# Moving a unit's mask to GpSimd, its steps to the end of a head pair, and a group's sums off VectorE

## The chip, the cores and the metric

One core of a Trainium2 chip runs the whole kernel in one launch. The metric is the device time of that core in microseconds (us); less is better. Engines are called as the profile calls them: PE (TensorE matmul), PEld (its weight loads), DVE (VectorE), ACT (ScalarE), POOL (GpSimd), SP (the engine that issues the DMAs). Each engine works through its own instructions in program order, and waits for the others by semaphores.

## The reference

Three stages follow each other: attention with a decay, an MLP with h·cos(h), and a mixture of experts whose gates are normalised by eight Sinkhorn rounds.

```python
def _attn_ref(q, k, v, f):                     # q, k, v: 4 x 8 x 576 x 64
    scores = scale * np.matmul(q, k.transpose(0, 1, 3, 2))
    cum = np.cumsum(np.log(np.clip(f, 0.0001, 1.0)), axis=-1)
    decay = cum[:, :, :, None] - cum[:, :, None, :]
    scores = np.where(causal, -1000000000.0, scores + decay)
    scores = scores - np.max(scores, axis=-1, keepdims=True)
    attn = np.exp(scores)
    attn = attn / (np.sum(attn, axis=-1, keepdims=True) + 1e-09)
    return np.matmul(attn, v)

def _moe_ref(x, w_in, w_out):                  # x: 2304 x 512, w_in: 512 x 2048
    h = x @ w_in
    return (h * np.cos(h)) @ w_out

def _moe2_ref(x, w_gate, w1, w2):              # 8 experts of width 1024
    P = np.exp(logits - logits.max())          # logits = x @ w_gate
    for _ in range(8):
        P /= P.sum(1, keepdims=True) + 1e-09
        P /= P.sum(0, keepdims=True) + 1e-09
        P *= N / E
    for e in range(E):
        out += P[:, e:e + 1] * (np.maximum(x @ w1[e], 0.0) @ w2[e])
    return out
```

## The kernel before, in words

The order of all work is written out by hand (`tc.manual_schedule()`): for each engine the program's order is the order in which Python issues instructions.

**Attention.** The 32 heads go in 16 pairs. A pair has seven steps (PS = 7), and the loop over x runs through them: step y = x % 7 works on three pieces of the first head's rows, three of the second's, and one with the last 64 rows of both. A step issues on PE transposes (`turn`, L699), scores three steps ahead (L642, L643), transposes of q and k of the next pair (L522) and products with v (`weigh`, L751, L731); on ACT the exponentials (L687), the high halves `A` (L713) and the high parts of q and k (L536, L538); on DVE the row limits `nm` (L681), the low halves `A` (L721), the low parts of q (L547) and the norms (L759 to L771); on POOL the low parts of k (L599, L552), the split of v (L503 to L507) and rows of the finished output (`split_row`, L242, L165, L166). Scores run as sums of products of high and low parts, so Q1 and Q2, K1 and K2 are the first and second operand of a head (four of each, in turn); `clear` fills the rows and columns that the heads leave empty with zeros and ones.

**Units.** The weights of the MLP come in 16 units, each with two halves of 128x512. They are raw double-precision words that are made into fp32 by integer work: `read_unit` has for each half three DVE steps (L189, L191, L194), a mask step that sets tiny values to zero (L197, with `dm`, the squared word from POOL, L175), and an ACT step that sums squares (L200). Then `scale_unit` adds up over the partitions (a matmul, L133, then L138 and three small POOL steps), and `split_unit` scales (ACT, L217) and splits into high and low halves (POOL, L165, L166). Units are Python generators: one `next(pieces)` goes one step further. Three and a half units are made during attention; the loop there decides at which x a step is taken (`turn_`), and `quiet` at which x a unit's matmul may go to PE. The other units are made between the items of the MLP.

**MLP.** An item is one 128-wide tile of the hidden layer for one chunk of tokens: 12 matmuls into `ph` (L281), ACT and DVE work (L296 to L312) that gives `H`, and two items later 12 matmuls with `H` into `a` (L1015). At the end of a block of items the four banks of `a` are emptied into `acc`, in the first block of the hidden layer by ACT (L1031).

**Experts.** Tokens go in three groups of 768. A group's operand is seven blocks of sums and differences (`combine`: sums L1424, high halves by ACT L1436, low halves by POOL L1439), planned at numbered hooks (`put_at`); 28 hooks make one group's pass through a layer pair. For the second group (p = 1) four of the eight sums run on DVE.

Of the kernel before, what the change touches and what calls it, by code (L numbers as in the profile page):

```python
# [17 lines left out]
ALU = mybir.AluOpType  # L18
# [5 lines left out]
def kernel(  # L24
# [13 lines left out]
    nc = tc.nc  # L38
# [9 lines left out]
    LAST = QT[-1][1]  # L48
# [26 lines left out]
    def f32(ap):  # L75
        return ap.bitcast(F32)
# [95 lines left out]
    def guard(n):  # L172
        if n < len(jobs):
            top = words_of(n)[2]
            nc.gpsimd.tensor_tensor(dms[n % 2], top, top, ALU.mult)  # L175

    def tm_of_unit(u):
        return u % 2 if u < NWA + 1 else (u - NWA + 1) % 3

    def read_unit(u):  # L180
        tm, ws = tmw[tm_of_unit(u)], wsum[u % 3]
        for half in range(2):
            n = 2 * u + half
            top, low, _ = words_of(n)
            x = tm[:, half * DM : (half + 1) * DM]
            xi = x.bitcast(I32)
            if n == 0:
                guard(0)
            nc.vector.tensor_scalar(xi, top, 3, 0x3FFFFFFF, ALU.logical_shift_left, ALU.bitwise_and)  # L189
            yield  # L190
            nc.vector.scalar_tensor_tensor(xi, top, -0x40000000, xi, ALU.bitwise_and, ALU.bitwise_or)  # L191
            guard(n + 1)
            yield
            nc.vector.scalar_tensor_tensor(xi, low, 29, xi, ALU.logical_shift_right, ALU.bitwise_or)  # L194
            load_job(n + 2)
            yield
            nc.vector.scalar_tensor_tensor(x, dms[n % 2], TINY * TINY, x, ALU.is_ge, ALU.mult)  # L197
            yield
            out_ = W[u % NSLOT][:, 0, half * DM : (half + 1) * DM] if late_[0] else junk[0][:, 0:DM]
            nc.scalar.activation(out_, x, AF.Square, accum_out=ws[:, half : half + 1])  # L200
        yield

    def scale_unit(u):
        while not quiet[0]:
            yield
        ps = total(wsum[u % 3], 0)
        if late_[0]:
            yield
        yield from make_scale(ps, sc_w[:, u], bk_w[:, u])
        nc.gpsimd.tensor_tensor(both[:, u : u + 1], bk_w[:, u, 0:1], bk_w[:, u, 1:2], ALU.mult)  # L210
        yield
# [12 lines left out]
        yield from scale_unit(u)  # L224
        yield from split_unit(u)

    late_, quiet = [False], [True]
    BATCHES = [(c0 // S, (c0 + n - 1) // S) for c0, n in CH]

    def chunk_scale(j):  # L230
# [84 lines left out]
    with tc.manual_schedule():  # L315

        with ExitStack() as actx:
# [83 lines left out]

            def clear(eng, i):
                other = QL[1 - i % 2]
                for t, rows_, value in (
                    (Q2, slice(D, P), 0.0), (K2, slice(D, P), 0.0), (Q2, slice(D, D + 4), -1.0), (K2, slice(D, D + 4), 1.0),
                ):
                    eng.memset(f32(t[i])[rows_, :], value)
                    yield
                for t in (Q1, Q2):
                    eng.memset(f32(t[i])[:, other : other + LAST], 0.0)  # L410

            def step(gen, n=1):
                for _ in range(n):
                    next(gen, None)
# [5 lines left out]
            nc.vector.memset(kraw[0][LAST:P, NQ - 1, :], 0.0)  # L420
            nc.vector.memset(quarter, 0.25)
            nc.vector.memset(shift, HALF_PI)
            step(clears[0], 2)
            make_identity(nc, ident)
            nc.gpsimd.memset(segm, 1.0)
            seg3 = segm.rearrange("p (g r) -> p g r", r=SEG)
# [5 lines left out]
                out=seg3, in_=seg3, compare_op=ALU.is_ge, fill=0.0, base=-1,  # L432
                pattern=[[SEG, NHEAD], [1, SEG]], channel_multiplier=-1,
            )
            step(clears[1], 5)


            nc.vector.tensor_scalar(fr, fr, 0.0001, 1.0, ALU.max, ALU.min)
# [10 lines left out]
            )  # L449
            nc.sync.dma_start(cumd.rearrange("r p s -> p r s"), f32(cum))  # L450
            step(clears[0])
            step(clears[2], 3)
            load_v(0)
            aug(0)
            load_pair(1)
# [14 lines left out]
            def pad_v(i):  # L470
                nc.gpsimd.memset(vraw[i][:, :, :, D : D + 1], 1.0)
                nc.gpsimd.memset(vraw[i][LAST:P, NQ - 1, :, :], 0.0)

            def pads():
                nc.gpsimd.memset(ones, 1.0)
                pad_v(0)
                nc.gpsimd.memset(qraw[1][0:LAST, NQ - 1, D : 2 * D], 0.0)
                nc.gpsimd.memset(qraw[1][LAST:P, NQ - 1, 0:D], 0.0)
                for t in (kraw[1], xpt):
                    nc.gpsimd.memset(t[LAST:P, NQ - 1, :], 0.0)  # L480
                for t in v_hi:
                    nc.gpsimd.memset(t[:, :, :, D : D + 1], 1.0)
# [391 lines left out]
            for x in range(-9, NSTEP + PS):  # L874
                for n, when in enumerate((NSTEP - 2, NSTEP + 1)):
                    if x == when:
                        ahead[n] = layer1(*items[n])
                quiet[0] = x % PS in (1, 2, 4, 5) or x >= NSTEP
                on_pe(x)
                if x == NSTEP + 2:  # L880
                    first = begin(*items[0], ahead[0])
                    core(first, None)
                    next(pieces, None)
                    core(None, first)
                    next(pieces, None)
                on_act(x)
                on_dve(x)
                if x == -7:
                    step(clears[2])
                go("pool", x)  # L890
                if x == -5:
                    pads()
                if x == -4:
                    step(clears[2])
                if x == -2:
                    more_pads()
                for j, (_, b1) in enumerate(BATCHES):
                    if x == (HP * b1 + HP - 1) * PS - 3:
                        scaling = chain(scaling, chunk_scale(j))
                turn_ = (x + 1) % 2 if x % PS != 3 else 0  # L900
                if x % PS == 4:
                    turn_ = 1
                if x >= 4 and (turn_ or x >= NSTEP - 8):
                    next(pieces, None)
                if x % 2 or x >= NSTEP - 8:
                    next(scaling, None)
                if rows and rows[0][0] <= x:
                    split_row(*rows.pop(0)[1:])
                if x == NSTEP - PS - 2:
                    block_factors(0)  # L910
                if x == NSTEP - PS - 1:
                    for u in range(NWA):
                        turn_factors(u, 0, 3)
                if x == NSTEP - 3:
                    assert not list(scaling)
                    for u in range(NWA):
                        turn_factors(u, 3, NCH)
                    down_factors(0, 0, NCH)
# [494 lines left out]
        def combine(p, rooms):  # L1413
# [6 lines left out]
                src[B11, k], src[B21, k], src[B22, k] = acc[:, k, t0], acc[:, 2 + k, t0], acc[:, 2 + k, t1]  # L1420

            def sub(dst, a, b):
                eng = nc.vector if p == 1 and k == 1 else nc.gpsimd
                return lambda: eng.tensor_tensor(dst, a, b, ALU.subtract)  # L1424

            sums = []
            for k in range(2):
# [12 lines left out]

            order = [(c, k) for c in (B11, B21, T2, T1, T3, B22, T4) for k in range(2)]
            if p == 1:
                order = [(c, k) for cs in ((B11, B21), (T2, T1), (B22, T3, T4)) for k in range(2) for c in cs]
            return sums, [high(*x) for x in order], [low_(*x) for x in order]

        def bank(kind):
# [248 lines left out]
        def plan_groups():  # L1695
            sums, highs, lo_ = combine(1, xtmp + [t[:, c : c + HN] for t in tmps for c in (0, DM)])
            for n, x in zip((1, 2, 4, 5), (0, 2, 1, 3)):
                put_at(n, lambda x=x: scale_group(1, x))
            for n, fn in zip((2, 3, 4, 5, 14, 15, 16, 17), sums):
                put_at(n, fn)  # L1700
            for n in range(14):
                put_at(10 + n, highs[n])
# [102 lines left out]
```

## Time and profile before

| | |
|---|---|
| median of 3 runs | 1970.86 us (1969.96 to 1970.99) |
| the profiled execution | 1973.44 us, its span 1971.7 us |
| busy in the span | PE 1930.4, DVE 1478.3, ACT 1214.0, POOL 1108.5 us |
| mean granted clock of TensorE | 0.996 |
| attention | about 13 to 242 us of the span |
| MLP | to about 636 us |
| experts | to the end |

The span runs from the first to the last instruction; the execution's own time is 1.74 us longer. Rows give start and duration; in brackets stands how long the engine sat idle before an instruction, and which engine's work ended that wait. "PEclk" is the clock granted to TensorE as a share of full speed (1.00 is the level of 2.4 GHz, 0.50 that of 1.2 GHz).

### The profile page before, as it was taken

Reading aid. Unit: us, or ns where it says so; the run is one execution under the profiler, and the core shown is the slowest. Engines: PE = TensorE matmul, PEld = TensorE weight load, DVE = VectorE, ACT = ScalarE, POOL = GpSimd, SP = SyncE. Lnnn points to the kernel's source line nnn. Section 1 sums busy time; section 2 is a strip of 40 time slices with the busy share of each in tenths; the row PEclk is TensorE's granted clock in tenths of the full one; section 3 lists DMA queues with packets and bytes.
Section 4 is the critical chain, followed back from the end, with each engine's and each line's share of the span. In section 5 each row is a group of like instructions: output and inputs, shape, how many; then the busy total and the mean of one; then the engine's idle time right before and its main releaser. Section 6 shows DMA issues by size and latency. Waiting matters only on the chain.

```text
span 1971.7 us, 38837 instructions
## 1 busy us (share of the span) xinstructions
PE 1930.4 (98%) x14490; PEld 1379.8 (70%) x14490; DVE 1478.3 (75%) x3271; ACT 1214.0 (62%) x2449; POOL 1108.5 (56%) x1546
## 2 busy tenths in 40 slices
PE   7999999999999999999999999999999999999998
PEld 6788855454455677777777777777777777777776
DVE  7888877787577678887777777777777777777776
ACT  6989888777644775655555555555555655556543
POOL 6778864333085785555555555555555555555531
PEclk8999999999999999999999999999999999999999
DMA  5454255453402022202122021220202202122022
GB/s 124 97 114 112 66 171 182 150 170 120 148 22 79 22 82 86 79 22 89 33 78 78 23 89 33 78 78 22 89 33 78 79 22 89 33 78 78 12 89 65
DMA packets 133916, 157.51 MB, mean 80 GB/s; under 512 B 63840, under 2 KB 98016, under 8 KB 133728
## 3 DMA queue, kind: packets, MB, share of 16 engines
q1 hardware_dynamic: 133728, 155.03, 25.8%
q8 instruction: 114, 1.87, 0.4%
q14 instruction: 74, 0.61, 0.1%
HBM read 139.71 MB, written 10.37 MB: 76 GB/s over the span
## 4 chain that ended last, share of the span: by engine, by line
PE 81%; DVE 8%; ACT 7%; issue 2%; DMA 1%; POOL 0%; SPq 0%; DVEq 0%; ACTq 0%; POOLq 0%
PE y L1670 19%; PE y L1549 18%; PE bq L1670 14%; PE bq L1549 14%; PE ph L281 6%; PE a L1015 6%; DVE A L721 1%; ACT E L687 1%; ACT A L713 1%; ACT seen L966 1%; DVE t L309 1%; DMA seen<-in_moe_w_dram 1%; DVE E L681 1%; PE pss L642 1%; ACT t L296 1%
## 5 line engine op out<-in xcount | busy, mean ns | idle before, releaser
L1670 PEld LDWEIGHTS <-h 128*128 128x128 f16 x6048 | 591.5, 98 | 74.9 <-issue 0.9
L1549 PEld LDWEIGHTS <-wa 128*128 128x128 f16 x4032 | 394.2, 98 | 257.1 <-issue 3.0
L1549 PE MATMUL y<-xc,wa 128*128 128x384 f16 x2304 | 429.6, 326 | 1.7 <-ACT ct L1565 1.0
L1584 POOL TENSOR_TENSOR h<-rt,h 128x384 f16<-128x384 f32 x192 | 175.4, 914 | 451.3 <-ACT h L1583 444.3
L1670 PE MATMUL y<-wb,h 128*128 128x256 f16 x3456 | 408.7, 273 | 0.0
L1565 ACT ACTIVATE ct<-y 128x384 f32<-128x384 f32 x192 | 94.4, 492 | 423.2 <-PE y L1549 423.0
L1549 PE MATMUL bq<-xc,wa 128*128 128x384 f16 x1728 | 327.9, 326 | 0.2 <-ACT ct L1565 0.2
L1670 PE MATMUL bq<-wb,h 128*128 128x256 f16 x2592 | 306.7, 273 | 0.2 <-DVE h L1575 0.2
L1651 DVE SCALAR_TENSOR_TENSOR acc<-y,gate,acc 128x256 f32<-128x256 f32 x504 | 212.7, 478 | 48.6 <-PE y L1670 48.6
L1015 PE MATMUL a<-H,w 128*128 128x512 f16 (+1 forms) x960 | 201.3, 358 | 4.0 <-DVE H L312 1.8
L281 PE MATMUL ph<-xt,w 128*128 128x512 f16 (+1 forms) x960 | 199.8, 358 | 0.0
L1651 DVE SCALAR_TENSOR_TENSOR acc<-bq,gate,acc 128x256 f32<-128x256 f32 x378 | 159.7, 478 | 39.2 <-PE bq L1670 39.1
L1015 PEld LDWEIGHTS <-w 128*128 128x128 f16 x960 | 93.4, 98 | 99.8 <-issue 7.8
L1575 DVE TENSOR_TENSOR h<-bq,h 128x384 f16<-128x384 f32 x288 | 158.2, 551 | 3.2 <-ACT h L1572 0.6
L1569 DVE SCALAR_TENSOR_TENSOR bq<-bq,ct 128x384 f32<-128x384 f32 x192 | 107.7, 561 | 65.2 <-PE bq L1549 64.4
L281 PEld LDWEIGHTS <-w 128*128 128x128 f16 x960 | 93.3, 99 | 88.8
L1569 DVE SCALAR_TENSOR_TENSOR bq<-y,ct 128x384 f32<-128x384 f32 x96 | 54.4, 566 | 122.1 <-PE y L1549 119.2
L1572 ACT CAST h<-bq 128x384 f16<-128x384 f32 x288 | 134.8, 484 | 14.2 <-DVE bq L1626 14.0
L1578 POOL TENSOR_TENSOR h<-st,h 128x384 f16<-128x384 f32 x96 | 87.9, 916 | 85.3 <-ACT h L1572 82.7
L309 DVE SCALAR_TENSOR_TENSOR t<-ph,turnv,t 128x512 f32<-128x512 f32 (+1 forms) x80 | 55.6, 695 | 96.1 <-ACT t L296 95.9
L1582 ACT ACTIVATE rt<-bq 128x384 f32<-128x384 f32 x192 | 93.8, 488 | 21.1 <-DVE bq L1569 18.4
L1327 POOL TENSOR_TENSOR tm<-sg 128x256 f32<-128x256 f32 x128 | 92.1, 731 | 13.5 <-POOL h L1578 12.3
(269 smaller groups left out, 3270.6 us busy)
## 6 DMA issues: line engine op xcount, KB each, us to landing
xc<-xd SPq DMA_DIRECT2D x105, 384.0 KB
seen<-in_moe_w_dram SPq DMA_DIRECT2D x64, 512.0 KB
sg<-in_moe_w_dram SPq DMA_DIRECT2D x64, 512.0 KB
stg<-in_moe_w_in_dram SPq DMA_DIRECT2D x16, 512.0 KB
stg<-in_moe_w_out_dram SPq DMA_DIRECT2D x16, 512.0 KB
xd<-xc SPq DMA_DIRECT2D x14, 384.0 KB
q<-q SPq DMA_DIRECT2D x30, 160.0 KB
out_dram<-acc SPq DMA_DIRECT2D x18, 256.0 KB
```

Of the source, the lines that this page charges most:

```text
L281: nc.tensor.matmul(ps[:, 0:n], w[:, ws, kk * P : (kk + 1) * P], XT[j][:, xs, kk, :], start=first, stop=kk == KD - 1 and (ws, xs) == PASSES ...
L1015: nc.tensor.matmul(a_of[b, j][x][:, 0:n], w[:, s1, DM + x * P : DM + (x + 1) * P], H[:, s2, 0:n], start=i == 0 and n_ == 0, stop=end and n ...
L1327: return [lambda o=o, x=x, y=y, op=op: nc.gpsimd.tensor_tensor(o, x, y, op) for o, x, y, op in todo]
L1549: nc.tensor.matmul(ps[:, 0:HN], w[:, ws, a, k, :], X[b][:, xs, k, :], start=fresh and n == 0, stop=n == 5, skip_group_check=not fresh,)
L1565: nc.scalar.activation(c, cut(ps), AF.Copy, scale=RAISE)
L1569: nc.vector.scalar_tensor_tensor(cut(c), cut(ps), RAISE, other, ALU.mult, ALU.add)
L1572: nc.scalar.copy(HT[m][c][:, 0, :], src)
L1575: nc.vector.tensor_tensor(HT[m][c][:, 1, :], src, HT[m][c][:, 0, :], ALU.subtract)
L1582: nc.scalar.activation(r, cut(ps), AF.Relu)
L1584: nc.gpsimd.tensor_tensor(HT[m][c][:, 1, :], r, HT[m][c][:, 0, :], ALU.subtract)
L1651: nc.vector.scalar_tensor_tensor(a, v, gate[:, tt, e : e + 1], a, ALU.mult, ALU.add)
L1670: nc.tensor.matmul(ps[:, at_ * HD : (at_ + 1) * HD], HT[m][a][:, s1, c * P : (c + 1) * P], W2T[side][m][:, s2, b, :], start=fresh and m == ...
```

## The change

Four edits are made at once.

1. The mask of a unit: DVE's one step (compare `dm` and multiply) becomes a comparison on POOL behind the squaring, and a multiplication on POOL, in all 32 halves.
2. A unit's steps during attention are taken at y = 4, 5, 6 of each pair and at y = 3 of each second pair; before it was each second x (with an exception at y = 3 and 4). The number of steps in two pairs stays seven. The unit's matmul for its scale is kept away from y = 4 (`calm`).
3. `clear` fills the empty columns of Q1 first, and for the fourth head of the first four this is done in `pads`, ahead of POOL's split of the first v.
4. The second group's four sums on DVE go to POOL, at hooks 14, 16, 18, 19 in place of 14 to 17, and the order in which this group's blocks are split is changed.

```diff
@@ guard
             nc.gpsimd.tensor_tensor(dms[n % 2], top, top, ALU.mult)
+            nc.gpsimd.tensor_scalar(dms[n % 2], dms[n % 2], TINY * TINY, 1.0, ALU.is_ge, ALU.mult)
@@ read_unit
-            nc.vector.scalar_tensor_tensor(x, dms[n % 2], TINY * TINY, x, ALU.is_ge, ALU.mult)
+            nc.gpsimd.tensor_tensor(x, dms[n % 2], x, ALU.mult)
@@ scale_unit
-        while not quiet[0]:
+        while not (quiet[0] and calm[0]):
@@ clear
                 other = QL[1 - i % 2]
+                eng.memset(f32(Q1[i])[:, other : other + LAST], 0.0)
+                yield
                 for t, rows_, value in (
...
-                for t in (Q1, Q2):
-                    eng.memset(f32(t[i])[:, other : other + LAST], 0.0)
+                eng.memset(f32(Q2[i])[:, other : other + LAST], 0.0)
...
-            step(clears[0], 2)
+            step(clears[0], 3)
...
-            step(clears[1], 5)
+            step(clears[1], 6)
...
-            step(clears[2], 3)
+            step(clears[2], 4)
@@ pads
                 pad_v(0)
+                step(clears[3])
@@ the loop over x
+                calm[0] = x % PS != 4 or x >= NSTEP
                 quiet[0] = x % PS in (1, 2, 4, 5) or x >= NSTEP
...
-                turn_ = (x + 1) % 2 if x % PS != 3 else 0
-                if x % PS == 4:
-                    turn_ = 1
-                if x >= 4 and (turn_ or x >= NSTEP - 8):
+                if x >= 4 and (x % PS >= 4 or x % (2 * PS) == 3 or x >= NSTEP - 8):
                     next(pieces, None)
@@ combine
             def sub(dst, a, b):
-                eng = nc.vector if p == 1 and k == 1 else nc.gpsimd
-                return lambda: eng.tensor_tensor(dst, a, b, ALU.subtract)
+                return lambda: nc.gpsimd.tensor_tensor(dst, a, b, ALU.subtract)
...
-                order = [(c, k) for cs in ((B11, B21), (T2, T1), (B22, T3, T4)) for k in range(2) for c in cs]
+                order = [(c, k) for cs in ((B11, B21), (B22,), (T2, T1, T3, T4)) for k in range(2) for c in cs]
@@ plan_groups
-            for n, fn in zip((2, 3, 4, 5, 14, 15, 16, 17), sums):
+            for n, fn in zip((2, 3, 4, 5, 14, 16, 18, 19), sums):
```

What moves is shown at three places. The first is POOL at the start of attention. Before, the split of the first v (its last instruction is `vl`) is followed by six fills of the fourth head's operands; `q_3_133` is the first operand Q1 of that head, `q_3_137` and `k_3_145` are the second ones.

```order
L507 TENSOR_TENSOR vl_150<-vrest,vh_148 128x512
L407 MEMSET q_3_137 64x640
L407 MEMSET k_3_145 64x576
L407 MEMSET q_3_137 4x640
L407 MEMSET k_3_145 4x576
L410 MEMSET q_3_133 128x64
L410 MEMSET q_3_137 128x64
```

Now the fill of `q_3_133` stands 12 instructions ahead of that `vl`, between the fills of the first v and of the second pair's raw q.

```order
L473 MEMSET vraw_152 128x10
L474 MEMSET vraw_152 64x130
L405 MEMSET q_3_133 128x64
L480 MEMSET qr_156 64x64
L481 MEMSET qr_156 64x64
```

The other five fills stay where they were. The second place is DVE in the second pair (x = 8 and 9, that is y = 1 and 2). Before, the third step of the first unit's first half (`tmw<-stg,tmw`) stood between the two low parts of q, ahead of the limit of 384 columns.

```order
L721 SCALAR_TENSOR_TENSOR A<-pst,A 128x384
L547 SCALAR_TENSOR_TENSOR q_0_130<-psq,q_0_130 64x576
L194 SCALAR_TENSOR_TENSOR tmw_73<-stg_71,tmw_73 128x512
L681 ISA E,nm<-pss,maskw 128x384
L681 ISA nm 128x1
L547 SCALAR_TENSOR_TENSOR q_1_131<-psq,q_1_131 64x640
L721 SCALAR_TENSOR_TENSOR A<-pst,A 128x512
```

Now nothing of a unit stands there; that step is one of three at the end of the first pair (y = 4 to 6), on either side of the limit of 384 columns there.

```order
L724 SCALAR_TENSOR_TENSOR A<-pst,A 128x512
L192 SCALAR_TENSOR_TENSOR tmw_73<-stg_71,tmw_73 128x512
L684 ISA E,nm<-pss,maskw 128x384
L684 ISA nm 128x1
L195 SCALAR_TENSOR_TENSOR tmw_73<-stg_71,tmw_73 128x512
L684 ISA E,nm<-pss,maskw 128x512
L684 ISA nm 128x1
```

The third place is POOL at the start of the MLP: a squaring `dm`, the split of unit 2's second layer of weights (`w<-tmw`), and a row of the attention's output (`acc`, `xt`). Before:

```order
L175 TENSOR_TENSOR dm_79<-stg_72 128x512
L165 TENSOR_SCALAR w_4462<-tmw_74 128x512
L166 TENSOR_TENSOR w_4462<-tmw_74,w_4462 128x512
L165 TENSOR_SCALAR w_4462<-tmw_74 128x512
L166 TENSOR_TENSOR w_4462<-tmw_74,w_4462 128x512
L242 TENSOR_SCALAR acc<-acc,scx 128x512
L165 TENSOR_SCALAR xt_84<-acc 128x512
L166 TENSOR_TENSOR xt_84<-acc,xt_84 128x512
L157 TENSOR_SCALAR turnv<-bkx,bkw 128x5
L175 TENSOR_TENSOR dm_78<-stg_71 128x512
```

Now a comparison (L176) stands behind each squaring, and the multiplication of the next unit's first half (L198, `tmw<-dm,tmw`) stands behind the row:

```order
L175 TENSOR_TENSOR dm_79<-stg_72 128x512
L176 TENSOR_SCALAR dm_79<-dm_79 128x512
L165 TENSOR_SCALAR w_4471<-tmw_74 128x512
L166 TENSOR_TENSOR w_4471<-tmw_74,w_4471 128x512
L165 TENSOR_SCALAR w_4471<-tmw_74 128x512
L166 TENSOR_TENSOR w_4471<-tmw_74,w_4471 128x512
L243 TENSOR_SCALAR acc<-acc,scx 128x512
L165 TENSOR_SCALAR xt_84<-acc 128x512
L166 TENSOR_TENSOR xt_84<-acc,xt_84 128x512
L198 TENSOR_TENSOR tmw_4477<-dm_78,tmw_4477 128x512
L157 TENSOR_SCALAR turnv<-bkx,bkw 128x5
```

The sum of squares on ACT that reads the multiplication's result keeps its place in ACT's order; before, it waited for DVE's mask step.

## Rows read from the trace of the kernel before

**Rows 1.** Busy times in a stretch of the MLP (columns as printed).

```profile
core 0: us, PE busy (x) PEld busy (x) DVE busy (x) ACT busy (x) POOL busy (x), PEclk, DMA share, GB/s
...
300.00:640.00 340.00, 337.68 (x1742) 172.93 (x1741) 243.34 (x414) 224.23 (x404) 149.21 (x213) 1.00 0.38 124
```

**Rows 2.** The same view for six head pairs, from norm to norm (same columns).

```profile
34.80:50.38 15.58, 13.92 (x147) 12.70 (x148) 13.55 (x41) 12.68 (x27) 9.48 (x12) 0.89 0.48 110
92.39:107.68 15.29, 13.69 (x146) 12.41 (x146) 13.46 (x40) 12.31 (x26) 10.79 (x16) 0.89 0.50 110
107.68:121.68 14.00, 13.17 (x151) 11.54 (x151) 12.98 (x43) 12.99 (x27) 11.82 (x15) 1.00 0.53 128
121.68:135.40 13.72, 13.18 (x152) 11.72 (x151) 11.31 (x38) 12.80 (x26) 10.35 (x21) 1.00 0.41 92
135.40:149.71 14.31, 12.99 (x148) 11.13 (x147) 12.98 (x40) 13.37 (x27) 13.12 (x17) 1.00 0.42 94
149.71:163.45 13.74, 12.14 (x145) 10.70 (x143) 13.29 (x40) 12.41 (x26) 10.70 (x16) 1.00 0.57 119
```

**Rows 3.** Timeline at the start of attention: start, us, what, idle before.

```profile
19.36 0.70 ACT L536 ACTIVATE q<-psq 64x640 fp32r<-64x640 f32 x1 [1.59 <-POOL q L410]
...
21.22 0.50 PE L642 MATMUL pss<-k,q 128*128 128x512 f32 x1 [1.50 <-DVE A L721]
```

**Rows 4.** PE's timeline: the same stretch of a step, in two pairs.

```profile
24.85 0.59 PE L642 MATMUL pss<-k,q 128*128 128x288 f32 x1
...
30.50 0.42 PE L642 MATMUL pss<-k,q 128*128 128x384 f32 x1
...
56.09 0.38 PE L642 MATMUL pss<-k,q 128*128 128x288 f32 x1
...
59.73 0.42 PE L642 MATMUL pss<-k,q 128*128 128x384 f32 x1
```

**Rows 5.** Timeline around the first unit's third step in the second pair.

```profile
37.67 1.20 DVE L194 SCALAR_TENSOR_TENSOR tmw<-stg,tmw 128x512 int32<-128x512 int32 x1
...
39.48 0.52 PE L699 MATMUL pst<-ident,E 128*128 128x128 f32 x3 [1.41 <-DVE nm L681]
```

**Rows 6.** Lines of the units over the span: duration ns min/median/max, first and last start.

```profile
L194 DVE SCALAR_TENSOR_TENSOR tmw<-stg,tmw x32: 680/692/1530, 37.7 to 462.4; 128x512 int32<-128x512 int32 x32
L197 DVE SCALAR_TENSOR_TENSOR tmw<-dm,tmw x32: 679/692/1449, 45.6 to 463.2; 128x512 f32<-128x512 bf16 x32
L165 POOL TENSOR_SCALAR w<-tmw x32: 607/617/1057, 79.4 to 488.8; 128x512 f16<-128x512 f32 x32
L166 POOL TENSOR_TENSOR w<-tmw,w x32: 1152/1159/1631, 80.1 to 489.5; 128x512 f16<-128x512 f32 x32
```

**Rows 7.** Timelines of POOL, ACT, DVE and PE at the start of the MLP.

```profile
259.48 1.47 POOL L166 TENSOR_TENSOR xt<-acc,xt 128x512 f16<-128x512 f32 x1
...
264.41 1.21 POOL L166 TENSOR_TENSOR xt<-acc,xt 128x512 f16<-128x512 f32 x1
...
259.70 0.61 ACT L200 ACTIVATE w<-tmw 128x512 f16<-128x512 f32 x1
...
262.06 0.48 ACT L306 CAST H<-ph 128x384 f16<-128x384 f32 x1 [1.09 <-DVE ph L305]
...
263.10 1.98 ACT L1031 ACTIVATE acc<-a,down 128x384 f32<-128x384 f32 x4
...
265.99 0.64 ACT L200 ACTIVATE w<-tmw 128x512 f16<-128x512 f32 x1
...
267.85 0.55 DVE L312 TENSOR_TENSOR H<-ph,H 128x384 f16<-128x384 f32 x1
...
263.71 2.11 PE L1015 MATMUL a<-H,w 128*128 128x384 f16 x12 [1.19 <-ACT acc L1031]
...
268.25 2.15 PE L1015 MATMUL a<-H,w 128*128 128x384 f16 x12
```

**Rows 8.** Start of the experts: two of DVE's four sums; PE's wait.

```profile
L1424 DVE TENSOR_TENSOR tm<-acc,tm x2: 1083/1174/1264, 656.0 to 659.1; 128x384 f32<-128x384 f32 x2
...
661.87 3.60 PE L1487 MATMUL bq<-acc,wgr 128*8 128x512 f32 x8 [1.52 <-DVE h L1575]
```

More of the change, by code (lines that the diff above doesn't have):

```diff
@@ L225, in run_unit @@
         yield from split_unit(u)
-    late_, quiet = [False], [True]
+    late_, quiet, calm = [False], [True], [True]
     BATCHES = [(c0 // S, (c0 + n - 1) // S) for c0, n in CH]
```

## The prediction

> **What bounds the kernel now.** First the busy times by engine: PE 1930 of a span of 1971.7 us, DVE 1478, ACT 1214, POOL 1109. PE is the bound, so a change can only gain where PE stands idle, or where its clock is low, and only loses where another engine makes PE late. The mean granted clock of 0.996 says that little is lost to the clock over the whole span, but not where; so I read the span in stretches.
>
> In the MLP the stretch view [rows 1] shows PE busy for 337.68 of 340.00 us. DVE and POOL have slack there (243 and 149 us busy), and whatever PE loses at this stage's edges is not regained inside it. In attention I read the same view from head pair to head pair [rows 2]. PE idles 0.5 to 1.9 us of each pair; pairs take 13.72 to 14.31 us at full clock, and two took 15.58 and 15.29 us at a mean clock of 0.89. Those two stand at the same place of the units' work as the last one shown (13.74 us at 1.00): they cost 1.84 and 1.55 us more, 3.4 together. Among the later pairs no other shows a low clock, but the start of attention does: from 24.85 to 30.50 PE needs 5.65 us for what takes 3.64 us at full clock [rows 4]. What PE waited for just ahead of it also stands there: ACT's high part of q waited 1.59 us for POOL's fill of that q, and then PE waited 1.50 us [rows 3]. The level there is 0.50, that is 1.2 GHz.
>
> The remaining waits that the change touches are at the edges between stages: POOL, ACT and DVE at the start of the MLP [rows 7], and PE's wait at the start of the experts [rows 8].
>
> **Clearing the fourth Q1 ahead.** The fill is on POOL behind the split of the first v; now it stands 12 instructions ahead of it. ACT's wait for it (1.59 us) ends; ACT is in the chain of this stretch, since PE's 1.50 us wait follows it through DVE's `A` [rows 3]. I take −1.6; the bounds are 0 (something else is as late) and −1.6. If PE isn't starved there, the half-clock stretch behind it goes as well: 5.65 − 3.64 = −2.0 [rows 4], bounds 0 and −2.0. I take −2.0, as the only long wait of PE ahead of the fall is this one. The same fill is only reordered for the other three heads, and what it delays there is a fill of one small block: 0.
>
> **The units' steps in attention.** Before, a step could fall at y = 1 or 2, where DVE also makes the two low parts of q. In the second pair L194 ran there for 1.20 us, and PE waited 1.41 us at 39.48 for the limit `nm` that was queued behind it [rows 5]; this is the pair that took 15.58 us. The pair from 92.39 has the same phase. With the steps at y = 4 to 6 nothing of a unit stands in that place. I count both excesses as gone: −3.4, bounds 0 (another wait makes the clock fall) and −3.4.
>
> Bunching has its own price: three steps stand in the last three steps of each pair, and a fourth at y = 3 in each second one. Of the full-clock pairs the shortest is the one with fewest DVE instructions (13.72 us, 38 of them), and the longest holds L189, L191 and the two ACT scales of a unit (14.31, with POOL at 13.12 of it) [rows 2]. A cycle of four pairs took 13.74 + 14.00 + 13.72 + 14.31 = 55.8 us. By their new contents I put the four at 14.0, 14.3, 13.7 and 14.0, which is 56.0; over the 3.5 cycles of attention that makes +0.8, and with the odd half cycle I take +1.0. The bounds are −3 (all pairs at 13.7: 3.5 × (55.8 − 54.9)) and +4 (two pairs of each cycle at 14.3 in place of 13.7 or 14.0).
>
> **The mask on POOL.** Two POOL instructions for a half replace one on DVE of 0.69 us [rows 6]. The comparison has the shape class of L165 (0.62 us). The multiplication with a bf16 and an fp32 operand and fp32 out has no row on POOL; the nearest are L166 on POOL (1.16, up to 1.63) and the same operands on DVE (0.69). I take 1.16, as it is a two-operand instruction on the same engine, and keep 0.69 and 1.63 as bounds. Eight halves are made in attention, two in each four pairs. POOL was busy 10.79 + 11.82 + 10.35 + 13.12 = 46.1 us in four pairs of 57.3 us [rows 2]; it gets 2 × (0.62 + 1.16) = 3.6 more, 49.7 of about 56, or 89 per cent. It still fits, and the instructions moved are covered by its idle time, so I cost them at 0 in attention; without this cover each half would put up to 1.8 us in front of the next pair's v split. DVE's 8 × 0.69 = 5.5 us are freed, but PE doesn't wait for DVE at most of those places, so that gains nothing by itself. Where POOL and DVE both work on two operands their instructions are sometimes longer: L194 takes 0.69 us at best and up to 1.53, L166 1.15 and up to 1.63 [rows 6].
>
> The Trainium skill (SBUF — State Buffer, section on the two separate sides; also Perfetto Trace Analysis, "Optimizing Scalar/DVE Operations") says that GpSimd shares a read port with VectorE, that an instruction holds it exclusively, and that moving work between these two "might not help". The spread of L194 above agrees with it; the sum is made without this rule.
>
> **The mask at the start of the MLP.** Here POOL is late already. ACT's Square at 259.70 now needs POOL's multiplication, which stands behind a row of the output (its last instruction ends at 259.48 + 1.47 = 260.95). With one comparison ahead of it (0.62) and itself (1.16) it ends at 262.7, so the Square comes 3.0 us later. Behind it on ACT are L306, which waited 1.09 us anyway, and L1031, which frees a bank of `a`; L1031 moves from 263.10 by 3.0 − 1.1 = 1.9, and PE's wait at 263.71 grows by as much. For the next half the row ends at 264.41 + 1.21 = 265.6; with two comparisons and two multiplications by then (3.6) the multiplication ends at 269.2 against a Square at 265.99: 3.2 us later. Behind that DVE's L312 of 267.85 and PE's products of 268.25 follow [rows 7]. The two delays overlap (the second holds the first): PE is late by 3.0. Bounds: 0, if POOL is ahead by then, as its order has slack in the last pairs; +5, if each adds by itself. In the rest of the MLP 24 halves move off DVE and onto POOL; 24 × 1.8 = 43 us fit into POOL's idle time there (191 of 340 us), and PE is full: 0.
>
> **The second group's sums.** Four sums leave DVE; two of them took 1.17 us on average, and PE waited 1.52 us for `h` from DVE behind them [rows 8]. Without them that wait shrinks: −1.5, bounds 0 and −2. POOL's four sums more are spread over hooks 14 to 19, and the new order of splits takes those sums last that are made last; 0.
>
> **The sum.** −1.6 − 2.0 − 3.4 + 1.0 + 3.0 − 1.5 = −4.5 us against the profiled execution of 1973.44, that is 1968.9; that execution lay 2.6 above the median of the runs, so in terms of the median 1970.86 − 4.5 = **1966.4**. Differences within 0.2% (3.9 us, 1966.9 to 1974.8) are about what a measurement of this kernel can't tell from no change, so the forecast lies close to that edge.
>
> **The rivals.** *The gains without the toll.* POOL has its last row of the output done earlier, as it isn't the last to finish in the last pairs, and the Square waits for nothing. Then the sum is −7.5, with bunching a little better −8: about 1963. For it: POOL's busy share at the end of attention leaves gaps. Against it: the row at 259.48 is issued late because its norms come late, which the change doesn't touch.
>
> *The clock falls stay.* The falls in the two pairs follow from PE's idle time, not from L194 alone, and the three bunched DVE steps stand against a POOL that is busy 89 per cent, with L194 at 1.2 to 1.5 us in place of 0.69. Then some other wait of 1.4 us makes PE fall to half clock as before; with −3.4 gone, and the toll paid: −1.1, about 1970. For it: two falls are shown, and each stands behind a wait of PE of 1.4 to 1.5 us [rows 3, 5].
>
> *POOL becomes the bound (slower).* POOL's queue holds v's split and the low parts of k of the next pair behind the multiplications. At 89 per cent any stretch of L166 and its like from 1.16 to 1.63 closes the rest: POOL has some 17 instructions a pair, and if six of them take 1.63 in place of 1.16, a pair gets 6 × 0.47 = 2.8 us more, 1.2 above its slack of 1.6 (14.0 less 49.7/4). Then PE waits for `vl` or the low parts of k, say in every second pair: 8 × 1.2 = +9.6 on the sum of −4.5, that is +5: 1976. It decides once POOL's busy time passes 14 us in two pairs in a row. Against it: the long ones are rare, as the medians of L165 and L166 stand at their minimum [rows 6].
>
> **How the numbers follow.** The forecast 0.45, the gains without the toll 0.22, the falls that stay 0.20, POOL as the bound 0.13. The range reaches from the bunching's better bound in the second case (1960) to the falls that stay with the toll's upper bound (1973.5). The forecast stands half a microsecond beyond the edge of 0.2%: it gives 0.28 to faster and 0.17 to the same; the second case is faster, the third the same: faster 0.50, same 0.37, slower 0.13.
>
> **What would show it.** ACT's high part of q without a wait at about 17.8 us; a clock of 1.00 from 24 to 30, and in the pairs from 35 and 92; no 1.4 us wait of PE for `nm` in the second pair; at the start of the MLP ACT's Square waiting some 3 us for POOL's multiplication, and PE's wait for L1031 at about 3 us in place of 1.19; PE's 1.52 us wait at the start of the experts gone. The prediction is wrong if the low clock turns up in other pairs, if the multiplication on POOL takes well over 1.2 us, or if PE waits for `vl` in attention.

## The result and the profile after

The changed kernel takes 1999.8 us (median of 4 runs, 1997.05 to 2000.67), the kernel before 1970.4 beside it: 1.0149 times as long, interval 1.0131 to 1.0166. That is 29 us slower, where 4.5 faster was forecast. The profiled execution took 2000.67 us, its span is 1998.9 us, 27.2 more than before. Of all runs below one, of the kernel with edits 3 and 4 alone, was an outlier at 9282.67 us; the ratio leaves it out, and without it that kernel's median would be 1967.06 in place of 1967.40.

The page's busy times point to an engine: GpSimd works 92.8 us more than before, TensorE 5.3 us more.

```profile
span 1998.9 us, 38848 instructions
...
PE 1935.7 (97%) x14490; PEld 1379.5 (69%) x14490; DVE 1463.2 (73%) x3235; ACT 1213.7 (61%) x2449; POOL 1201.3 (60%) x1614
```

The groups of GpSimd's instructions (busy us, mean ns, idle before) show the two new ones. The multiplication takes 1187 ns on average, near the 1.16 us taken. The comparison takes 2052 ns where 0.62 was taken.

```profile
L176 POOL TENSOR_SCALAR dm<-dm 128x512 bf16<-128x512 bf16 x32 | 65.7, 2052 | 2.8
...
L198 POOL TENSOR_TENSOR tmw<-dm,tmw 128x512 f32<-128x512 bf16 x32 | 38.0, 1187 | 7.5 <-DVE tmw L195 5.6 <-DVE rw L984 1.5 <-DVE gm L976 0.2
```

Edit 3 did what was foreseen. In the timelines ACT's q stands 1.54 us earlier than in [rows 3] and waits for nothing, and the two matmuls of [rows 4] are 3.18 us apart in place of 5.65: the clock didn't fall there.

```profile
17.82 0.70 ACT L539 ACTIVATE q<-psq 64x640 fp32r<-64x640 f32 x1
...
23.08 0.38 PE L645 MATMUL pss<-k,q 128*128 128x288 f32 x1
...
26.26 0.42 PE L645 MATMUL pss<-k,q 128*128 128x384 f32 x1
```

But in the second pair GpSimd makes two comparisons before it gets to the last instruction of v's split. PE waited 3.17 us for it, and the clock fell with that wait (the stretch view: PEclk 0.76 from 33.00 to 36.15, 0.50 from 36.15 to 39.00).

```profile
28.12 2.28 POOL L176 TENSOR_SCALAR dm<-dm 128x512 bf16<-128x512 bf16 x1
...
31.85 1.04 POOL L175 TENSOR_TENSOR dm<-stg 128x512 bf16<-128x512 f32 x1
32.98 1.93 POOL L176 TENSOR_SCALAR dm<-dm 128x512 bf16<-128x512 bf16 x1
34.98 1.12 POOL L510 TENSOR_TENSOR vl<-vrest,vh 128x512 f16<-128x512 f32 x1
...
36.15 0.21 PE L754 MATMUL pv<-vl,A 128*128 128x64 f16 x1 [3.17 <-POOL vl L510]
```

In the last pair the eighth half goes the whole way late: comparison, v's split, multiplication, ACT's sum of squares, PE's matmul for the scale.

```profile
236.70 2.27 POOL L176 TENSOR_SCALAR dm<-dm 128x512 bf16<-128x512 bf16 x1
...
241.62 1.16 POOL L198 TENSOR_TENSOR tmw<-dm,tmw 128x512 f32<-128x512 bf16 x1
...
242.81 0.63 ACT L201 ACTIVATE sq<-tmw 128x512 bf16<-128x512 f32 x1 [3.32 <-POOL tmw L198]
...
243.58 0.38 PE L133 MATMUL pv<-wsum,ones 128*128 128x2 f32 x2 [1.47 <-ACT sq L201]
```

At the start of the MLP the place of [rows 7] reads so: POOL's multiplication at 274.17, ACT's Square that waits 3.95 us for it, behind it L1032 that empties a bank, and PE 4.33 us late for that bank (before: 1.19).

```profile
274.17 1.16 POOL L198 TENSOR_TENSOR tmw<-dm,tmw 128x512 f32<-128x512 bf16 x1
...
275.36 0.63 ACT L201 ACTIVATE w<-tmw 128x512 f16<-128x512 f32 x1 [3.95 <-POOL tmw L198]
...
277.85 1.98 ACT L1032 ACTIVATE acc<-a,down 128x384 f32<-128x384 f32 x4
...
278.46 1.76 PE L1016 MATMUL a<-H,w 128*128 128x384 f16 x5 [4.33 <-ACT acc L1032]
```

The clock falls there too (same columns as rows 1, PEclk third from the right):

```profile
275.00:280.00 5.00, 1.54 (x5) 0.69 (x5) 1.95 (x4) 4.32 (x10) 4.65 (x6) 0.70 0.24 92
280.00:285.00 5.00, 5.00 (x18) 2.14 (x17) 1.10 (x3) 2.96 (x7) 4.75 (x5) 0.62 0.35 105
```

The waits of ACT from 257 to 407 us add this up: eight times for the multiplication, 15.9 us in all.

```profile
ACT w L201 <- POOL tmw L198: 15.9, 8, 4.3
```

Edit 4: the instruction of PE that waited 1.52 us in [rows 8] waits no more.

```profile
688.81 3.60 PE L1487 MATMUL bq<-acc,wgr 128*8 128x512 f32 x8
```

### The profile page after: what moved, and what is told of

It reads as the page before. It is cut to its first block, busy times and chain, and to the rows that moved or that the text cites. A ratio compares the mean times of both kernels' runs of the same rounds, so it can differ in the third digit from the quotient of the medians.

```text
span 1998.9 us, 38848 instructions
## 1 busy us (share of the span) xinstructions
PE 1935.7 (97%) x14490; PEld 1379.5 (69%) x14490; DVE 1463.2 (73%) x3235; ACT 1213.7 (61%) x2449; POOL 1201.3 (60%) x1614
## 4 chain that ended last, share of the span: by engine, by line
PE 80%; POOL 6%; DVE 4%; ACT 4%; issue 3%; DMA 2%; SPq 0%; DVEq 0%; POOLq 0%; ACTq 0%
PE y L1670 19%; PE y L1549 18%; PE bq L1670 14%; PE bq L1549 14%; PE ph L282 6%; PE a L1016 5%; POOL dm L176 1%; PE pst L702 1%; DMA seen<-in_moe_w_dram 1%; PE pv L754 1%; POOL k L555 1%; DMA stg<-in_moe_w_in_dram 1%; POOL tmw L198 1%; POOL dm L175 1%; PE pss L645 1%
```

## The experiments

My theory after the result (A) was that the comparison on GpSimd is what costs: GpSimd comes late with the splits of v and with what ACT and PE wait for. The rival was that the bunched steps (edit 2) cost it.

**1. What a comparison costs on GpSimd.** In the kernel before, behind the last squaring, on free buffers (an excerpt, the ten instructions measured):

```diff
+            g.tensor_scalar(b0, f0, TINY * TINY, 1.0, ALU.is_ge, ALU.mult)
+            g.tensor_scalar(b0, b0, TINY * TINY, 1.0, ALU.is_ge, ALU.mult)
+            g.tensor_scalar(b0, b0, 1.0, 0.0, ALU.mult, ALU.add)
+            g.tensor_scalar(f1, b0, TINY * TINY, 1.0, ALU.is_ge, ALU.mult)
+            g.tensor_scalar(f1, b0, 1.0, 0.0, ALU.mult, ALU.add)
+            g.tensor_scalar(f1, f0, TINY * TINY, 1.0, ALU.is_ge, ALU.mult)
+            g.tensor_scalar(f1, f0, 1.0, 0.0, ALU.mult, ALU.add)
+            g.tensor_scalar(f1, f0, TINY * TINY, None, ALU.is_ge)
+            g.tensor_scalar(f1, f0, 0.0, 1.0, ALU.max, ALU.min)
+            g.tensor_tensor(f1, b0, f0, ALU.mult)
```

> The kernel before, with ten instructions of 128x512 added on GpSimd once, behind the last squaring of a unit, on buffers that are free by then. They are the comparison in four combinations of bf16 and fp32, plain multiplications and conversions of the same shapes, and the multiplication bf16 x fp32. Theory A (comparing is what is slow): every comparison takes about 2 us, whatever the type, and the plain forms stay at 0.6 to 0.7. Theory B (bf16 as both source and result is slow): the bf16 to bf16 forms take about 2 us with either operation, and a comparison from fp32 to fp32 takes about 0.7. The multiplication bf16 x fp32 takes 1.2 by both.

The timeline of GpSimd, in the diff's order:

```profile
455.85 1.95 POOL L181 TENSOR_SCALAR dm<-stg 128x512 bf16<-128x512 f32 x1
457.88 1.92 POOL L182 TENSOR_SCALAR dm<-dm 128x512 bf16<-128x512 bf16 x1
459.88 0.80 POOL L183 TENSOR_SCALAR dm<-dm 128x512 bf16<-128x512 bf16 x1
460.76 2.24 POOL L184 TENSOR_SCALAR stg<-dm 128x512 f32<-128x512 bf16 x1
463.08 0.62 POOL L185 TENSOR_SCALAR stg<-dm 128x512 f32<-128x512 bf16 x1
463.78 1.92 POOL L186 TENSOR_SCALAR stg<-stg 128x512 f32<-128x512 f32 x1
465.78 0.62 POOL L187 TENSOR_SCALAR stg<-stg 128x512 f32<-128x512 f32 x1
466.48 1.49 POOL L188 TENSOR_SCALAR stg<-stg 128x512 f32<-128x512 f32 x1
468.06 1.94 POOL L189 TENSOR_SCALAR stg<-stg 128x512 f32<-128x512 f32 x1
470.08 1.16 POOL L190 TENSOR_TENSOR stg<-dm,stg 128x512 f32<-128x512 bf16 x1
```

The operation sets the price, not the type: 1.92 to 2.24 us for each comparison with two operations, 1.49 with one, 1.94 for a maximum and minimum, 0.62 to 0.80 for multiply and add. (The 2.24 and the 0.80 stand beside a step of VectorE; see the last section.) Theory A's reading holds, theory B's falls.

**2. Edit 1 alone, and the change without it.** The first is the kernel before with the two lines of edit 1. The second is the changed kernel with the mask given back (an excerpt):

```diff
-            nc.gpsimd.tensor_scalar(dms[n % 2], dms[n % 2], TINY * TINY, 1.0, ALU.is_ge, ALU.mult)
-            nc.gpsimd.tensor_tensor(x, dms[n % 2], x, ALU.mult)
+            nc.vector.scalar_tensor_tensor(x, dms[n % 2], TINY * TINY, x, ALU.is_ge, ALU.mult)
```

> The kernel before with the mask on GpSimd alone (edit 1); the steps stay at their old places. Theory A (the long comparison on GpSimd makes it late for what others wait for): +20 to +35 us against the kernel before, most of it lost between 230 and 450 us of the span. Rival (the bunched steps make it late): 0 to +5 us.

> The changed kernel with the mask given back to VectorE: edits 2, 3 and 4 are left. Theory A: the loss is gone and the gains of the start of attention (-3.4 us) and of the experts' sums (-1.4) show, 1964 to 1968 us. Rival (bunched steps): 1985 to 2000 us.

Alone: 1999.07 us, 1.0144 times the kernel before (1.0128 to 1.0159). Without it: 1969.69 us, 0.9991 (0.9982 to 1.0000). The mask on GpSimd is the whole loss, and the rival falls. Edit 1 alone is behind the profiled execution of before by 6.2 us at 232 us of the span, by 20.6 at about 450 and by 24.1 at the start of the experts, as theory A had it. The way differs with the places of the steps: in attention PE waited there only 0.9 us for GpSimd, but ACT's sum of squares waited 7.8 us for the multiplication. The second is 1.7 us above my range: edit 2 isn't free.

**3. Edits 3 and 4, and edit 2, by themselves.**

> The kernel before with edits 3 and 4 alone (the fill ahead, the second group's sums on GpSimd). By the trace of the changed kernel -1.5 to -2.0 us for the fill at the start of attention, and -1.4 for the sums: 1966 to 1968 us. If the gain at the start of attention came from the steps' new places and not from the fill, about 1969.

> The kernel before with edit 2 alone (the steps at the end of a pair), against 1970.9. By the difference of the two kernels already run (1969.69 less 1967.40): +2, 1973. If the steps only pay by themselves where the start of attention is still at half clock, as the prediction had it: -1 to -2.

Edits 3 and 4: 1967.40 us, 0.9977 (0.9968 to 0.9986), as expected. Edit 2 alone: 1975.16 us, 1.0020 (1.0011 to 1.0029), a loss of 3.7 us (1971.47 beside it), more than expected. On top of edits 3 and 4 it costs 2.3 us (1969.69 less 1967.40). Two stretches show where it gains and where it loses. With the steps bunched the clock of the second pair stays up (first fence, edits 2 to 4), without edit 2 it is 0.89 as before (second fence, edits 3 and 4):

```profile
35.00:50.00 15.00, 14.27 (x167) 12.50 (x166) 14.34 (x44) 14.55 (x30) 10.61 (x13) 1.00 0.44 97
...
221.79:229.14 7.35, 5.43 (x71) 4.69 (x72) 7.18 (x24) 4.46 (x10) 4.69 (x7) 1.00 0.14 41
```

```profile
35.00:50.00 15.00, 14.14 (x147) 12.88 (x148) 13.13 (x41) 12.01 (x24) 8.04 (x12) 0.89 0.61 139
...
221.92:227.72 5.80, 5.55 (x73) 4.74 (x72) 5.63 (x22) 4.72 (x10) 4.15 (x7) 1.00 0.28 93
```

The last row of each is the second half of a late pair, between its two norms. There DVE was already busy 5.63 of 5.80 us. It held one step of a unit (0.68 us). Now it holds three, DVE is busy 7.18 of 7.35 us, and the half is 1.55 us longer. The three in DVE's timeline of the kernel with edits 2 to 4:

```profile
223.80 0.68 DVE L191 SCALAR_TENSOR_TENSOR tmw<-stg,tmw 128x512 int32<-128x512 int32 x1
...
225.55 1.22 DVE L194 SCALAR_TENSOR_TENSOR tmw<-stg,tmw 128x512 int32<-128x512 int32 x1
...
227.93 0.69 DVE L197 SCALAR_TENSOR_TENSOR tmw<-dm,tmw 128x512 f32<-128x512 bf16 x1
```

**4. The price of the comparison.** The changed kernel with a cheap operation in its place (first added line; the guard against tiny values is then left out), and with the one-operation comparison (second; two runs):

```diff
-            nc.gpsimd.tensor_scalar(dms[n % 2], dms[n % 2], TINY * TINY, 1.0, ALU.is_ge, ALU.mult)
+            nc.gpsimd.tensor_scalar(dms[n % 2], dms[n % 2], 0.0, 1.0, ALU.mult, ALU.add)
+            nc.gpsimd.tensor_scalar(dms[n % 2], dms[n % 2], TINY * TINY, None, ALU.is_ge)
```

> The changed kernel with the comparison on GpSimd replaced by a multiplication with 0 and an addition of 1 (the guard against tiny values is left out, everything else stays): about 0.7 us in place of 2.0, which is the price that the prediction took. Theory A (the comparison's price is what failed): 1966 to 1972 us. Rival (a second two-operand instruction in GpSimd's queue is enough to make the rows and splits late, whatever the comparison takes): 1982 us or more.

> The changed kernel with the comparison written with one operation (without the multiplication by 1.0), which took 1.49 us in place of 1.92 to 2.24 in the probe. Theory A: between the two others, with 32 x 0.5 us less on GpSimd some 7 to 12 us under the changed kernel: 1987 to 1993 us. Rival (price without weight): 1998 to 2000.

1977.10 us (1.0028, 1.0016 to 1.0039) and 1994.27 us (1.0117, 1.0103 to 1.0131). The first lies between theory and rival, the second just beyond its range. GpSimd's two instructions take 1.9, 2.8 and 3.2 us for a half in these two and in the changed kernel, and cost 7.4, 24.6 and 30.1 us against the kernel with the mask back: the loss isn't in proportion. At the price that the prediction took, the mask still costs 1977.1 − 1969.7 = 7.4 us; the price adds 1999.8 − 1977.1 = 22.7. ACT's waits for the multiplication, in the same stretch of the MLP, grow with it (cheap; the changed kernel's 15.9 stand above):

```profile
ACT w L201 <- POOL tmw L198: 7.3, 5, 3.0
```

**5. Busy time or wait?** The comparison stays on GpSimd and the multiplication goes back to VectorE's old step.

```diff
-            nc.gpsimd.tensor_tensor(x, dms[n % 2], x, ALU.mult)
+            nc.vector.scalar_tensor_tensor(x, dms[n % 2], TINY * TINY, x, ALU.is_ge, ALU.mult)
```

> The changed kernel with the multiplication back on VectorE (the old mask step, which compares once more), but with the comparison still on GpSimd behind the squaring: GpSimd keeps 2.05 us more for each half, and no other engine waits for a multiplication of it. Theory A1 (GpSimd's busy time makes its splits, rows and low parts late): by the kernels with 1.9, 2.7 and 3.2 us more per half (+7, +25, +30 against the same without), +8 to +11 against 1969.7, that is 1978 to 1981 us. Rival A2 (it is the multiplication, behind which the sum of squares waits, that makes the loss): 1970 to 1973 us.

1975.32 us (1.0020, 1.0010 to 1.0029), 5.6 above the kernel without the comparison: between the two. GpSimd's occupation alone makes part of the loss, but the same 2 us for each half cost less than I derived from the others. (VectorE reads what the comparison writes, but was never idle for it.) The comparison without the multiplication costs 5.6 us, the multiplication with a cheap operation ahead of it 7.4; together they make 13 of the 30. So the wait for the multiplication has a part too; how the two divide the 30 us isn't settled, as they grow together.

**6. Where: attention or the MLP.** Edit 1 for the first seven halves alone, all made in attention (an excerpt; the multiplication has the same condition):

```diff
+            if n < 7:
-            nc.gpsimd.tensor_scalar(dms[n % 2], dms[n % 2], TINY * TINY, 1.0, ALU.is_ge, ALU.mult)
+                nc.gpsimd.tensor_scalar(dms[n % 2], dms[n % 2], TINY * TINY, 1.0, ALU.is_ge, ALU.mult)
```

> The changed kernel with the mask on GpSimd for the first seven halves alone, those made in attention; the other 25 as before on VectorE. By the places of the delays in the two traces (14.6 us up to the first products of the MLP, 16.3 in it) the delay of attention is kept in full and the MLP adds at most the part at its start: 1983 to 1988 us. If the MLP gives back what attention lost, or loses the same whatever happens ahead of it: under 1977, or over 1995.

1977.42 us (1.0033, 1.0021 to 1.0046), 7.7 above the kernel with the mask back, half of what I expected. By the starts of the last norm the seven halves cost attention 7.2 us (4.2 behind the kernel before, in place of 3.0 ahead of it), and that stays. Of the other 7.4 of the 14.6 us that I had put down to them, some 6 arise from the 29th norm to the last one, with the eighth half, whose rows stand above. The other 1.3 are there from the second pair on, where the two kernels are the same: that is the difference of two executions.

**7. What freeing VectorE can give, and other places for the steps.** The mask left out on every engine (tiny values stay); the steps at their old places from x = 63 on; and the steps at y = 3, 4, 6 (and 5 in each second pair), the last two with the mask on VectorE (an excerpt of the third):

```diff
-                if x >= 4 and (x % PS >= 4 or x % (2 * PS) == 3 or x >= NSTEP - 8):
+                if x >= 4 and (x % PS in (3, 4, 6) or x % (2 * PS) == 5 or x >= NSTEP - 8):
```

> The changed kernel with the mask left out altogether: no comparison and no multiplication, on no engine (tiny values aren't set to zero; the squaring stays). It shows the most that taking the mask off VectorE can give. If VectorE is full in the second half of a pair, as the trace with the mask on VectorE and the bunched steps shows it (7.18 of 7.35 us), 1 to 3 us under that kernel's 1969.7: 1966.5 to 1968.5. If VectorE's mask step was off the path, the same 1969.7.

> Edits 2, 3 and 4 with the mask on VectorE, but the steps at their old places from the tenth pair on (x = 63). In the trace with edits 2, 3 and 4 the lead over the kernel before grew to 7.9 us up to there and shrank to 3.0 by the end of attention, in the one with edits 3 and 4 it stayed at 4 to 5. If the places in the late pairs cost this: a lead of about 7 at the end of attention and 1964 to 1965 us. If it is a chance of phases that any other order has too: 1966 to 1969.

> Edits 2, 3 and 4 with the mask on VectorE, but the steps at y = 3, 4 and 6 of each pair and at y = 5 of each second one: as many steps, one less in the second half of a pair. If a full VectorE in that half is what the bunching costs: 1967 to 1968.5 us, with a lead at the end of attention of 4 to 6 us in place of 3.0. If it is not, the same 1969.7, or slower where the step at y = 3 now collides with the first half's end.

Without a mask: 1963.73 us (0.9965, 0.9953 to 0.9978), 6.0 below the kernel with the mask back and more than I expected. At the last norm it is 6.75 us ahead of the kernel before, in place of 2.98: VectorE's mask step was on the path of the bunched pairs, and 2.2 of the 6 us come behind attention. Switched back: 1967.06 us (0.9979, 0.9970 to 0.9987), in the rival's range; it is 5.2 ahead at the last norm, not 7. Steps at 3, 4, 6: 1971.52 us (1.0006, 0.9997 to 1.0015), 1.8 above the kernel with the mask back, where 1 to 3 below were expected. It was 7.1 us ahead at the first norm of the 15th pair, 2.5 better than the bunched one, as a full VectorE would have it, and lost 5.6 from there to the last norm; the stretch view shows the clock at 0.87 there. What made it fall in that order I didn't settle, so that a full VectorE is the whole price of the bunching isn't shown.

The kernel with edits 3 and 4 alone and the one switched back are the fastest complete ones; the two can't be told apart.

A table of the lead (−) or lag (+) over the kernel before, in us, as the difference of the starts of the same instruction: the first DVE instruction of a norm, and PE's router product of [rows 8]. Each kernel is one execution here. The last row says how far two executions differ without any change: the probe's attention is that of the kernel before, and it leads by up to 3.4 us, as the profiled execution of before was a long one (2.6 us above its median).

| kernel | 2nd norm | 4th | 19th | 30th | last | router |
|---|---|---|---|---|---|---|
| changed | −3.4 | −0.7 | +0.7 | +6.8 | +11.6 | +26.9 |
| one-operation comparison | −3.5 | −3.9 | −3.3 | +1.6 | +6.9 | +19.1 |
| cheap operation | −3.4 | −5.3 | −6.8 | −4.3 | −1.3 | +3.4 |
| mask back (edits 2, 3, 4) | −3.4 | −5.7 | −7.9 | −3.0 | −3.0 | −4.0 |
| edits 3 and 4 | −4.5 | −4.4 | −5.1 | −4.4 | −4.4 | −5.6 |
| edit 1 alone | −2.8 | −4.2 | −0.6 | +6.2 | +6.3 | +24.1 |
| probe of experiment 1 | −1.2 | −2.6 | −3.4 | −2.7 | −2.7 | (behind the probe) |

## Why the prediction was wrong

**The step that failed** is the price in "The comparison has the shape class of L165 (0.62 us)". I gave the multiplication two bounds and the comparison none, because its shape stands in a row; but that row's operation is multiply and add, and no comparison on GpSimd stands in any row of before. It took 2.05 us. A half then costs GpSimd 3.2 us, not 1.8. Of the miss of 33.4 us (1999.8 less 1966.4) this price makes 22.7, the rest of the mask 4.4 (7.4 in place of 3.0) and the steps 4.7 (+2.3 in place of −2.4).

**"Still fits, 0 in attention" and "the rest of the MLP: 0".** Both failed at the real price. I compared busy sums: 89 per cent of four pairs, 43 of 191 idle us in the MLP. Work that others wait for in a fixed order isn't covered by idle time elsewhere. In attention PE's waits for the last part of v's split and for the low parts of k grew from 2.9 us (second fence, the mask back on VectorE) to 14.8 (first fence, the changed kernel):

```profile
PE pv L754 <- POOL vl L510: 9.5, 10, 3.2
PE pss L646 <- POOL k L555: 5.3, 6, 1.1
```

```profile
PE pv L753 <- POOL vl L509: 2.7, 3, 0.9
PE pss L645 <- POOL k L554: 0.2, 1, 0.2
```

Between the changed kernel and the one with the mask back lie 14.6 us up to the first products of the MLP, some 5.5 at its start, and 10.8 in the rest of it. At the low price the same three places hold 1.7, 3.5 and 2.2 us (cheap operation against mask back), 7.4 in all against the +3.0 of the sum. So the two zeros were off by about 2 us each by themselves, and by 14.6 and 10.8 with the real price.

**DVE's freed 5.5 us, "gains nothing by itself"**: wrong too. With the mask on no engine the kernel is 6.0 us faster than with the mask on VectorE. Against that, GpSimd's two instructions cost 36 us (1999.8 less 1963.7), not 30.

**The start of the MLP**, +3.0: right in place and mechanism (multiplication, Square, L1032, PE). At the price that I took the lag there grows by 3.7 us from the first products to the eighth item's, at the real one by 5.7 (by the starts of those products).

**The steps**, −3.4 + 1.0: wrong in sign, with +2.3 measured. The −3.4 was read from one execution of the kernel before, and I took its two falls of the clock for a fixed cost. In the probe of experiment 1 attention is unchanged and PE waits the same 1.41 us for `nm` in the second pair (at 38.37), yet the clock stays at 1.00 there, and at the start it is 0.72 where that of [rows 4] was 0.50:

```profile
24.00:30.00 6.00, 5.69 (x53) 5.59 (x54) 4.43 (x17) 3.59 (x8) 2.75 (x6) 0.72 0.51 112
35.00:50.00 15.00, 13.34 (x163) 12.12 (x162) 14.34 (x41) 13.65 (x29) 9.02 (x12) 1.00 0.46 110
```

The fall in the pair from 92 us shows in no other execution, with the steps at their old places neither (edits 3 and 4 alone):

```profile
92.00:108.00 16.00, 14.10 (x157) 12.26 (x158) 15.23 (x44) 13.97 (x29) 12.16 (x16) 1.00 0.67 140
```

That in the second pair is there with edits 3 and 4 and gone with edits 2 to 4, as forecast; that the new places end it isn't shown, as it can be gone without them. The price of bunching reached my upper bound of +4: from the 19th norm to the last the kernel with edits 2 to 4 loses 4.9 us of its lead, that with edits 3 and 4 0.7, so 4.2 between them. I had put whole pairs at 13.7 to 14.3 us; the second half of a pair, with VectorE full in it, was the stage to read.

**The fill ahead**, −1.6 − 2.0, **and the sums**, −1.5: right in their sum. By its ratio of 0.9977 the kernel with edits 3 and 4 is 4.5 us faster, against 5.1. The −1.6 shows as a lead of 1.63 us at the first norm (0.01 the other way in the probe), and the router's wait of 1.52 is gone. The −2.0 depends on the execution: in the four kernels without the fill ahead the clock from 24 to 30 is 0.50, 0.50, 0.72 and 1.00, in the ten with it always 1.00.

**The rivals.** "POOL becomes the bound" is in part what happened, and at the place it named (`vl`), but not for its reason: GpSimd's L166 was not stretched, its median stayed at 1.16 us and its longest on `w` fell from 1.63 to 1.47. Its sign, GpSimd busy for over 14 us in two pairs in a row, came only in the last two pairs (15.23 and 14.88), and the loss in the MLP it didn't name:

```profile
222.52:238.93 16.41, 13.07 (x149) 11.01 (x148) 14.65 (x45) 12.23 (x26) 15.23 (x17) 1.00 0.23 60
238.93:255.84 16.91, 12.99 (x131) 10.83 (x128) 8.44 (x30) 8.64 (x18) 14.88 (x32) 0.90 0.07 26
```

That its 1976 is close to what the cheap operation gave (1977.1) is chance: there the mask cost attention 1.7 us, where the rival had 9.6. "The clock falls stay" is half right: the fall of the second pair stayed in the changed kernel, behind a new wait.

## What to carry to other kernels

A price is taken from a row of the same engine and the same operation; where only the shape agrees, it is an unknown with two bounds, and a probe of ten instructions settles it. Work given to an idle engine is costed by its place in that engine's order and by who waits behind it, not by the engine's idle share: here the idle share nearly covered 1.9 us a half, and not 2.8. A loss to the clock that one execution shows is looked for in a second one before it is booked as a gain. Look for the half of a period in which an engine is already full before placing steps into it.

## What the hardware showed unexpectedly

A comparison with two operations cost GpSimd three times a multiply and add on the same 512 columns: 1.92 against 0.62 us, with bf16 and with fp32. A maximum and minimum, measured once in fp32, took 1.94. In the probe, the 2.24 and the 0.80 stand where a two-operand step of VectorE ran on into them, for 0.45 and 0.32 us; with the cheap operation, bf16 to bf16, 20 of the 32 took 0.62 to 0.67.

In the changed kernel 11 of the 32 comparisons took 2.24 to 2.28 us, the others 1.92 to 2.02. In each of the 11 a unit's step of VectorE with two tensor operands was under way at the start and ran on for 0.45 to 0.46 us of it. Each of these steps had itself begun during the squaring ahead (L175) and ended 0.55 us after it; the one below took 1.19 us. Of the 19 steps of a unit with two tensor operands that started inside a comparison, 15 took their usual 0.68 or 0.69. One comparison of each kind (first fence), and the VectorE step beside it (second fence):

```profile
221.05 2.27 POOL L176 TENSOR_SCALAR dm<-dm 128x512 bf16<-128x512 bf16 x1
...
265.09 1.95 POOL L176 TENSOR_SCALAR dm<-dm 128x512 bf16<-128x512 bf16 x1
```

```profile
220.32 1.19 DVE L195 SCALAR_TENSOR_TENSOR tmw<-stg,tmw 128x512 int32<-128x512 int32 x1
...
265.61 0.68 DVE L195 SCALAR_TENSOR_TENSOR tmw<-stg,tmw 128x512 int32<-128x512 int32 x1
```

The Trainium skill (SBUF — State Buffer, section on the two separate sides) has the one that starts first hold the shared port for its whole instruction. The trace agrees where the squaring or VectorE started first (the comparison grew by 0.33 of the 0.46 us), and doesn't show it where the comparison did.
